# Start-up of a fused layernorm, scan and feed-forward kernel: other transposes in place of dummy matmuls, one copy on another engine, and a new order of the weight passes

## The chip, the cores and the metric

One core of one Trainium2 chip runs the whole program. The metric is the time of one execution on the device in microseconds (us), median of several runs. The profile belongs to one of the runs, and its clock starts with the span, which is some 1.3 us shorter than the time of the run.

## The reference, cut to what matters

```python
def reference(A_x, ..., B_w_gate, B_w_up, B_w_down):     # x: 1 x 2048 x 512, bf16
    def _A_ref(x, ...):            # diagonal complex state space model, P = 512
        Bu = einsum("bld,pd->blp", x + 0j, B_bar)
        h_t = Lam_bar * h_(t-1) + Bu_t                    # over 2048 steps
        return 2.0 * einsum("blp,dp->bld", hseq, Cmat).real + x * Dskip
    def _B_ref(x, w_gate, w_up, w_down):                  # F = 1376
        return (_gelu(x @ w_gate) * (x @ w_up)) @ w_down
    xn = _layernorm(A_x, axis=-1)
    return A_x + _A_ref(xn, ...) + _B_ref(xn, B_w_gate, B_w_up, B_w_down)
```

The 2048 rows go through in four blocks of four tiles (128 rows each). The change concerns only the first block, and of that only the first seven chunks of 128 columns of w_gate and w_up.

## The kernel before: the parts that the change touches

The program must start with TensorE while data is still coming in. Tile j of x is centred (the mean taken off, by VectorE), turned (four 128 x 128 transposes on TensorE into a PSUM bank), copied to SBUF, and then multiplied by the weights. The contraction over 512 is cut in four passes k = 0..3, because the weights arrive in four slices. `ks(k, j, w)` is pass k of tile j; `fill(n)` issues n small dummy matmuls, which stand in the queue so that TensorE stays active while it waits.

```python
        for k in range(KD):                       # loads, on the sync engine's queue
            if k in (1, 3):
                ld_x0((k + 3) // 2)               # x tiles 2 and 3
            ld_wk(WG, WGc, ins["B_w_gate"], k)    # slice k: 128 x 512, 128 KB
            ld_wk(WU, WUc, ins["B_w_up"], k)
# ... cut ...
        def cent_T(j, k0, k1, bank, eng="A", c0=0):          # turn, then copy
            ...
            PE(f, 56.0 * (k1 - k0), [XNp[j][k0 > 0] if j < 2 else XN[j], IDN], [BANK[bank]], "T0")
            ...
            if eng == "A":
                GATE["evTA"] = ACT(lambda e: e.activation(dst, src, ACTF.Copy, scale=sc), ...)
                return GATE["evTA"]
            return V(lambda e: e.tensor_scalar(dst, src, sc, None, ALU.mult), ...)
# ... cut ...
        ch(V(lambda e: e.tensor_reduce(SUM0.ap, X[0].ap, ...)))
        ch(cent(0, 0), cent(0, 1))
        fill(1)
        ch(cent_T(0, 0, 1, 7, "V"))
        ch(cent(1, 0), cent(1, 1))
        fill(4)
        # ks(k, j, w): pass k of tile j, for both column groups
        ks(0, 0, [0], True)
        cent_T(1, 0, 1, 6)
        ks(0, 0, [1])
        cent_T(0, 1, 4, 7)
        ks(0, 1, [0], True)
        cent_T(1, 1, 4, 5)
        ks(0, 1, [1])
        for j in range(2):
            ks(1, j, [0, 1])
        # ... statistics of tiles 0 to 3 on VectorE ...
        cent_T(2, 0, 4, 7)
        for j in range(2):
            ks(2, j, [0, 1])
        for k in range(3):
            ks(k, 2, [0, 1], k == 0)
        for j in range(3):
            ks(3, j, [0, 1])
            for u in range(2):
                GT_evac(j, u, acc(j, u))
            if j == 0:
                cent_T(3, 0, 4, 6)
        # then GT_mm: whole groups of four passes, later weights all there
```

After this block come, for every four tiles, the rest of the gate and up projection (GU), the state space input (BU), and the down projection (DN). GU and BU read x turned by DMA transposes (`TR`), not by TensorE.

## Time and profile before

| | before |
|---|---|
| time, median of 3 runs | 177.21 us (177.15 to 177.61) |
| span of the profiled run | 175.7 us |
| TensorE busy | 98% of the span, 98% of the chain that ended last |
| first real matmul | 4.57 us |
| start of pass k=1 / k=2 / first whole group | 6.06 / 7.42 / 11.10 us |

TensorE works almost without a hole. So the time can be read as three terms: the moment at which TensorE enters its unbroken stretch (the first whole group, line L711 before and L712 after), the work from there on, and whatever waits turn up in that stretch.

### The profile page before, as it was taken

What the parts mean: (1) busy time and instruction counts of PE and PEld (TensorE: products, weight loads), DVE (VectorE), ACT (ScalarE), POOL (GpSimd) and SP (SyncE); (2) the same over time, 40 slices, a digit from 0 to 9 for tenths busy, and PEclk for the clock granted to TensorE, in tenths of its full rate; (3) what the DMA queues carried; (4) which work ended last, traced back from release to release, by engine and by line L of the source; (5) the groups of instructions that cost most, each with busy time, mean ns of one, the idle gap of its engine ahead of it and who ended that gap; (6) DMA issues with size and microseconds to landing.
All of it is one profiled execution on the core that took longest, in us unless ns stands there. A gap on an engine that the chain in (4) does not pass through costs nothing.

```text
span 175.7 us, 2494 instructions
## 1 busy us (share of the span) xinstructions
PE 172.1 (98%) x868; PEld 84.0 (48%) x883; DVE 159.8 (91%) x279; ACT 95.5 (54%) x185; POOL 10.7 (6%) x24
## 2 busy tenths in 40 slices
PE   8999999999999999999999999999999999999995
PEld 3545564644544444444644444444464444444454
DVE  6987999996999989889899999989999899999941
ACT  5476677899876898383576792000667970000000
POOL 3122030201000000002100000000000000000000
DMA  5899999695998000002015000002001000000311
GB/s 155 241 320 174 215 178 222 126 132 113 191 298 225 0 4 2 0 30 85 8 39 111 1 0 0 4 0 90 30 0 30 4 0 0 0 0 0 120 64 60
DMA packets 32420, 14.36 MB, mean 82 GB/s; under 512 B 23736, under 2 KB 32408, under 8 KB 32408
## 3 DMA queue, kind: packets, MB, share of 16 engines
q1 hardware_dynamic: 32240, 14.07, 35.5%
q8 instruction: 7, 0.11, 0.3%
q10 hardware_dynamic: 168, 0.13, 0.2%
q14 instruction: 5, 0.04, 0.1%
HBM read 6.46 MB, written 2.10 MB: 49 GB/s over the span
## 4 chain that ended last, share of the span: by engine, by line
PE 98%; issue 1%; DVE 0%
PE PS L883 37%; PE PS L842 32%; PE PS L748 16%; PE PS L711 4%; PE PS L700 3%; PE PS L816 3%; PE PS L932 2%; PE PS L679 1%; PE PS L939 0%; DVE arena L901 0%
## 5 line engine op out<-in xcount | busy, mean ns | idle before, releaser
L883 PE MATMUL PS<-arena 128*128 128x512 bf16 (+3 forms) x317 | 65.9, 366 | 0.3
L842 PE MATMUL PS<-arena 128*128 128x512 bf16 x257 | 57.1, 379 | 0.4
L883 PEld LDWEIGHTS PS<-arena 128*128 128x128 bf16 (+1 forms) x323 | 30.8, 98 | 35.2
L842 PEld LDWEIGHTS PS<-arena 128*128 128x128 bf16 x264 | 25.8, 98 | 30.2
L786 DVE TENSOR_TENSOR_SCAN arena<-arena 128x512 bf16<-128x512 f32 x32 | 38.9, 1255 | 0.0
L857 ACT ACTIVATE arena<-PS 128x512 bf16<-128x512 f32 x33 | 19.8, 599 | 25.8 <-DVE arena L901 16.7
L748 PE MATMUL PS<-arena 128*128 128x512 bf16 (+1 forms) x134 | 28.0, 366 | 0.1
L861 ACT ACTIVATE arena<-PS 128x512 bf16<-128x512 f32 x33 | 19.8, 600 | 5.1 <-PE PS L842 5.1
L875 ACT ACTIVATE PS<-arena 128x512 f32<-128x512 bf16 (+2 forms) x17 | 9.6, 581 | 19.7 <-DVE arena L901 19.0
L748 PEld LDWEIGHTS PS<-arena 128*128 128x128 bf16 x136 | 13.3, 98 | 14.1
L757 ACT ACTIVATE arena<-PS 128x512 bf16<-128x512 f32 x32 | 17.7, 592 | 2.1 <-PE PS L748 2.1
L901 DVE TENSOR_TENSOR arena<-PS,arena 128x512 bf16<-128x512 f32 (+2 forms) x17 | 10.9, 653 | 6.4 <-PE PS L883 6.4
L863 DVE TENSOR_TENSOR arena<-arena 128x512 bf16<-128x512 bf16 x33 | 13.1, 416 | 1.7 <-ACT arena L861 1.6
L775 DVE TENSOR_TENSOR arena<-arena 128x4096 bf16<-128x4096 bf16 (+1 forms) x5 | 9.2, 1859 | 0.8 <-ACT arena L606 0.8
L773 DVE TENSOR_TENSOR arena<-arena 128x4096 bf16<-128x4096 bf16 (+1 forms) x5 | 9.2, 1859 | 0.1
L798 DVE TENSOR_TENSOR arena<-arena 128x4096 bf16<-128x4096 bf16 x4 | 9.2, 2288 | 0.1
L799 DVE TENSOR_TENSOR arena<-arena 128x4096 bf16<-128x4096 bf16 x4 | 9.1, 2284 | 0.0
L720 ACT ACTIVATE arena<-PS,arena 128x256 bf16<-128x256 f32 (+1 forms) x16 | 6.6, 448 | 3.9 <-PE PS L700 2.1
L610 DVE BATCH_NORM_STATS2 arena<-arena 128x6 f32<-128x512 bf16 x12 | 7.7, 679 | 0.1
L711 PE MATMUL PS<-arena 128*128 128x512 bf16 (+1 forms) x40 | 7.1, 336 | 0.0
L723 DVE SCALAR_TENSOR_TENSOR arena<-PS,arena 128x256 bf16<-128x256 f32 (+1 forms) x16 | 6.3, 445 | 0.5 <-PE PS L700 0.5
L700 PE MATMUL PS<-arena 128*128 128x512 bf16 (+1 forms) x28 | 6.2, 349 | 0.2
(96 smaller groups left out, 124.6 us busy)
## 6 DMA issues: line engine op xcount, KB each, us to landing
out_dram<-arena SPq DMA_DIRECT2D x15, 128.0 KB, 1.7
arena<-in_A_x_dram SPq DMA_DIRECT2D x3, 512.0 KB, 5.3
arena<-in_B_w_down_dram SPq DMA_DIRECT2D x1, 1280.0 KB, 7.2
arena<-in_B_w_gate_dram SPq DMA_DIRECT2D x4, 128.0 KB, 3.0
arena<-in_B_w_up_dram SPq DMA_DIRECT2D x4, 128.0 KB, 3.1
arena<-in_B_w_gate_dram SPq DMA_DIRECT2D x1, 480.0 KB, 6.5
arena<-in_B_w_up_dram SPq DMA_DIRECT2D x1, 480.0 KB, 7.4
arena<-arena SPq DMA_TRANSPOSE x25, 3.1
```

Of the source, the lines that this page charges most:

```text
L700: PE(lambda e: e.matmul(dst, XCd(j, k), WGU[:, ws[0]:ws[-1] + 1, k, f0:f1], start=first, stop=k == KD - 1, skip_group_check=True), d_pe([w ...
L711: ins_ = e.matmul(dst, XCd(j, k), WGU[:, :, k, f0:f1], start=(k == 0), stop=(k == KD - 1))
L748: ins_ = e.matmul(PS[bank][:, 128 * j0:128 * j1], BBT[c][dk].ap[:, 128 * s:128 * (s + 1)], XNT[b].ap[:, dk, 128 * j0:128 * j1], start=(dk ...
L757: GATE["evBu"] = ACT(lambda e, bank=bank, k3=k3, s=s, c=c: e.activation(SSc[k3][s][c].ap, PS[bank][:, :], ACTF.Copy), d_act(512), [BANK[ba ...
L786: V(lambda e, g=g, rb=rb, init=init: e.tensor_tensor_scan(g.ap, rb, g.ap, init, ALU.mult, ALU.add), d_dve_scan(512), [g, PA[RRr]] + ([CARc ...
L842: ins_ = e.matmul(PS[bank][0:m, c0:c1], W.ap[:, dk, 128 * ft:128 * ft + m], XNT[b].ap[:, dk, c0:c1], start=(dk == 0), stop=(dk == KD - 1))
L857: GATE["last_gelu"] = ACT(lambda e, bg=bg, kk=kk, m=m: e.activation(GG[kk].ap[0:m, :], PS[bg][0:m, :], ACTF.Gelu_apprx_tanh), d_act(512), ...
L861: ACT(lambda e, bu=bu, kk=kk, m=m: e.activation(UPB[kk].ap[0:m, :], PS[bu][0:m, :], ACTF.Copy), d_act(512), [BANK[bu]], [UPB[kk]], "evU")
L863: V(lambda e, kk=kk, m=m, ft=ft, k2=k2: e.tensor_tensor(HTt[k2][ft].ap[0:m, :], GG[kk].ap[0:m, :], UPB[kk].ap[0:m, :], ALU.mult), d_dve_tt ...
L875: ACT(lambda e: e.activation(PS[bank][:, c0:c1], X[tt].ap[:, c0:c1], ACTF.Copy), d_act(c1 - c0), [X[tt]], [BANK[bank]], "seed")
L883: ins_ = e.matmul(PS[bank][:, c0:c1], l_[:, 128 * j:128 * (j + 1)], r_[:, c0:c1], start=False, stop=last and n == len(ops) - 1, skip_group ...
L901: V(lambda e: e.tensor_tensor(OUTB[ko].ap[:, c0:c1], PS[bank][:, c0:c1], XD[tt].ap[:, c0:c1], ALU.add), d_dve_1x(c1 - c0), [BANK[bank], XD ...
```

## The change

Its intent is to keep TensorE on useful work while the first tiles and weights arrive: transposes that are needed anyway replace dummies, VectorE is relieved of a copy, and tile 2 is made ready early enough to fill the wait ahead of pass k=2.

```diff
+        fill(2)
+        cent_T(0, 0, 1, 7)                 # copy now by ScalarE
+        ch(cent(1, 0), cent(1, 1))
         fill(1)
-        ch(cent_T(0, 0, 1, 7, "V"))
-        ch(cent(1, 0), cent(1, 1))
-        fill(4)
+        ev0 = cent_T(0, 1, 4, 5, True)
+        ev1 = cent_T(1, 0, 1, 6)
+        S.order_behind(ev0(), ev1)
         ks(0, 0, [0], True)
-        cent_T(1, 0, 1, 6)
         ks(0, 0, [1])
-        cent_T(0, 1, 4, 7)
+        cent_T(1, 1, 4, 7)
         ks(0, 1, [0], True)
-        cent_T(1, 1, 4, 5)
         ks(0, 1, [1])
-        for j in range(2):
-            ks(1, j, [0, 1])
-        ch(*stats(0, 2)); ch(sub(2)); ch(*stats(0, 0)); ch(*stats(0, 1))
+        ch(*stats(0, 2)); ch(sub(2))
+        ks(1, 0, [0, 1])
+        cent_T(2, 0, 1, 6)
+        cent_T(2, 1, 4, 7)
+        ks(1, 1, [0, 1])
+        ks(0, 2, [0, 1], True)
+        ch(*stats(0, 0)); ch(*stats(0, 1))
 ... cut: statistics, norms ...
-        cent_T(2, 0, 4, 7)
-        for j in range(2):
+        ks(1, 2, [0, 1])
+        for j in range(3):
             ks(2, j, [0, 1])
-        for k in range(3):
-            ks(k, 2, [0, 1], k == 0)
         for j in range(3):
-            ks(3, j, [0, 1])
+            GT_k(3, j, 0, [0, 1])
+            if j == 0:
+                cent_T(3, 0, 4, 6)
+            GT_k(3, j, 1, [0, 1])
             for u in range(2):
                 GT_evac(j, u, acc(j, u))
-            if j == 0:
-                cent_T(3, 0, 4, 6)
 ... cut: banks of the first two groups of tile 3 swapped ...
```

More of the change, by code (lines that the diff above doesn't have):

```diff
@@ L671, in build, with cent_T @@
         XNp = [[Buf("XN%d_%d" % (j, n), "sb", XN[j].lo + 256 * n, XN[j].lo + (1024 if n else 256)) for n in range(2)] for j in range(2)]
-        def cent_T(j, k0, k1, bank, eng="A", c0=0):
-            pt = PS[bank].bitcast(BF16)[:, c0:c0 + 128 * (k1 - k0)]
+        def cent_T(j, k0, k1, bank, later=False):
+            pt = PS[bank].bitcast(BF16)[:, 0:128 * (k1 - k0)]
             def f(e):
@@ L684, in cent_T, with evac @@
             sc = 1.0 if j else 1.0 / D
-            if eng == "A":
+            def evac():
                 GATE["evTA"] = ACT(lambda e: e.activation(dst, src, ACTF.Copy, scale=sc), d_act(128 * (k1 - k0)), [BANK[bank]], w, "evT")
                 return GATE["evTA"]
-            return V(lambda e: e.tensor_scalar(dst, src, sc, None, ALU.mult), 110 + 0.6 * 128 * (k1 - k0), [BANK[bank]], w, "evT")
+            return evac if later else evac()
         FR = ((0, 256), (256, 512), (512, 768), (768, 896))
@@ L994, in build @@
         TR(0, [0, 1])
-        cent_T(2, 0, 4, 7)
-        for j in range(2):
+        ks(1, 2, [0, 1])
+        for j in range(3):
             ks(2, j, [0, 1])
-        for k in range(3):
-            ks(k, 2, [0, 1], k == 0)
         for j in range(3):
-            ks(3, j, [0, 1])
+            GT_k(3, j, 0, [0, 1])
+            if j == 0:
+                cent_T(3, 0, 4, 6)
+            GT_k(3, j, 1, [0, 1])
             for u in range(2):
                 GT_evac(j, u, acc(j, u))
-            if j == 0:
-                cent_T(3, 0, 4, 6)
         for (j, u), bank in zip([(3, 0), (3, 1), (0, 2), (0, 3), (1, 2), (1, 3), (2, 2), (2, 3), (3, 2), (3, 3)],
-                                (7, 6, 0, 1, 2, 3, 4, 5, 0, 7)):
+                                (6, 7, 0, 1, 2, 3, 4, 5, 0, 7)):
             GT_mm(j, u, bank)
```

## The prediction

> **What bounds the kernel now.** I read the page first, then the chain that ended last, then the timelines of matmuls (PE) and weight loads (PEld) in the first 12 us, which is all the change touches, and last the issue and landing of the weights' DMAs.
>
> ```profile
> PE 172.1 (98%) x868; PEld 84.0 (48%) x883; DVE 159.8 (91%) x279; ACT 95.5 (54%) x185; POOL 10.7 (6%) x24
> ...
> PE 98%; issue 1%; DVE 0%
> ```
>
> TensorE is busy for 98% of the span and carries 98% of the chain. So only three things shorten this kernel: less TensorE work, fewer TensorE stalls, a shorter tail. From 7.42 us on the chain is TensorE without a break; its pieces of 0.05 us "issue" are holes of one missing record (883 weight loads, 868 matmuls). What the change can win lies before that:
>
> ```profile
> 4.46 0.11 issue
> 4.57 0.38 PE PS L700 x2
> ...
> 7.34 0.08 issue
> 7.42 2.75 PE PS L700 x12
> ```
>
> The merged weight loads show where TensorE waits (bracket: idle before it, and what ended it):
>
> ```profile
> 4.54 0.13 PEld L700 LDWEIGHTS PS<-arena 128*128 128x128 bf16 x2 [0.26 <-issue]
> ...
> 5.37 0.11 PEld L700 LDWEIGHTS PS<-arena 128*128 128x128 bf16 x2 [0.15 <-ACT arena L686]
> ...
> 6.03 0.13 PEld L700 LDWEIGHTS PS<-arena 128*128 128x128 bf16 x2 [0.16 <-issue]
> ```
> ```profile
> 7.39 0.13 PEld L700 LDWEIGHTS PS<-arena 128*128 128x128 bf16 x2 [0.23 <-issue]
> ```
>
> "issue" hides two causes. At 6.03 it is the second ScalarE copy (5.42 to 5.91). At 7.39 it is a DMA: L700 accumulates over four passes (the code's steps k = 0..3), pass k needs slice k of both weights, and here pass k=2 begins. Issue and time to landing of the "up" slices k = 1, 2, 3:
>
> ```profile
> 3.07 0.43 SPq L484 DMA_DIRECT2D arena<-in_B_w_up_dram  x1
> ...
> 4.02 0.43 SPq L484 DMA_DIRECT2D arena<-in_B_w_up_dram  x1
> ...
> 5.45 0.43 SPq L484 DMA_DIRECT2D arena<-in_B_w_up_dram  x1
> ```
> ```profile
> arena<-in_B_w_up_dram SPq DMA_DIRECT2D x1, 128.0 KB, 2.8
> ```
> ```profile
> arena<-in_B_w_up_dram SPq DMA_DIRECT2D x1, 128.0 KB, 3.3
> ```
> ```profile
> arena<-in_B_w_up_dram SPq DMA_DIRECT2D x1, 128.0 KB, 3.8
> ```
>
> These landed at about 5.84, 7.29 and 9.25 us. Pass k=2 started at 7.42, that is 0.13 us after its slice. So **the start-up is paced by the weights' arrival**, and the next arrival is close too:
>
> ```profile
> 9.36 0.10 PEld L700 LDWEIGHTS PS<-arena 128*128 128x128 bf16 x1
> ```
>
> This is the first weight load of pass k=3. It ran 0.11 us after slice 3 landed; the loads that really stalled on a semaphore pair ran 0.10 us after it (7.39 after 7.29). Pass k=3 has almost no room.
>
> ```profile
> 7.42 2.75 PE L700 MATMUL PS<-arena 128*128 128x512 bf16 x12
> 10.01 0.39 PE L679 MATMUL PS<-arena 128*128 128x128 bf16 x4
> 10.23 1.03 PE L700 MATMUL PS<-arena 128*128 128x512 bf16 x4
> ```
>
> From these starts a 512-wide matmul takes (10.01-7.42)/12 = 0.216 us of TensorE, a turn (128x128 transpose) 0.22/4 = 0.056 us, a 256-wide one 0.109 us. Pass k=3 is the eleventh matmul after 7.42: 7.42 + 10 x 0.216 = 9.58 us.
>
> **What the Trainium skill says.** (1) "TensorE: Matmul & The Clock Gate", Part 1: the array starts at half clock and is released by some 3.4 us of sustained activity, on a free-running window. The trace agrees: the dummies of L932 are 0.427 us apart, twice 0.216, and the small dummies go from 0.107 to 0.074 us apart at 4.2 us, 3.4 us after the first. (2) The same page, Part 2, says LDWEIGHTS are pulled ahead of running matmuls. The trace agrees: the load at 9.36 starts with the matmul before its own. So a late semaphore costs only what exceeds one matmul. (3) The same page, Part 4: a transpose takes about 275 ns in a kernel and does not count as activity the same way. Here one lasts 218 to 286 ns from start to end; whether it counts no view shows. This speaks against swapping dummies for turns. (4) "ScalarE: Activation LUTs", What ACT_TABLE_LOAD costs: an activation with immediates takes 186 ns + 0.833 ns per element, 293 ns for 128. The trace has 277 for the copy, and 225 for VectorE's copy of the same shape.
>
> **The change, part by part.**
> - Dummies: five become three. Two go, each 0.107 us at the cold clock, but the three other turns of tile 0 and the first of tile 1 fill that time. The first real matmul waits for the copy of tile 0's first turn, not for dummies, so nothing is won directly.
> - That copy moves to ScalarE: +0.05 us (277-225), and about +0.05 us because a second dummy now stands ahead of the turn (it starts near 3.93, not 3.87). The first L700 matmul goes from 4.57 to about 4.67. Against that VectorE is free sooner, so tile 1 is centred by about 4.4 instead of 4.81.
> - Pass k=0 then runs without the wait of 0.15 us at 5.37: 4.67 + 8 x 0.109 + 3 turns 0.17 = 5.71 us. But slice 1 allows pass k=1 only at 5.84 + 0.13 = 5.98 (before: 6.06). Won: 0.08 us; 0.27 us are stall.
> - Tile 2's turns go ahead of k=2, with pass 0 and 1 of tile 2 (four 512-wide): 5.98 + 0.43 + 0.22 (turns) + 0.43 + 0.86 = 7.93 us. Pass k=2 starts there, after slice 2 (7.29), so **the 0.25 us wait at 7.42 goes**. Its six matmuls end at 7.93 + 1.29 = 9.22 us.
> - The work ahead of pass k=3 is the same as before (three passes for three tiles, 12 turns), only reordered. TensorE is ready at 9.22 instead of 9.58, 0.36 us sooner. But slice 3 landed at 9.25, and a stalled load plus its matmul follows 0.135 us after (7.29 to 7.42): 9.39 us. **Won: 9.58 - 9.39 = 0.19 us; the other 0.17 us become a new wait.**
> - Tile 3's turns one matmul sooner: before, their copy ended at 11.03 and the next group started at 11.10, with no stall but no room. If only pass k=3 came 0.19 sooner, this copy would be the limit. With the change the turns start at 9.60, the copy runs about 10.03 to 10.63, and the group starts at 9.39 + 1.29 + 0.22 = 10.90 without a wait. Cost: none; it protects the 0.19.
> - After that nothing is removed. In before, the L711 loads have at least 0.6 us of room to their weights (landed 11.94), the L842 loads after them 0.8 us, and the ones that wait for DMA transposes later 0.56 us. An advance of 0.19 us survives to the end, where TensorE drives the tail.
>
> Sum: 177.21 - 0.19 = 177.02 us, 0.1%.
>
> **Rivals.**
> 1. *All stalls go.* From 4.57 us on they sum to 0.15 + 0.07 + 0.03 + 0.25 = 0.50 us; this would give 176.7. Against it: the DMA queue issues without waits until 7.5 us, so no engine can make slices 1 and 3 come sooner. Room above my 0.19 exists only if slice 3 lands earlier in those runs; TensorE's own limit is 0.36 us (176.85).
> 2. *The wait only moves.* If slice 3 lands 0.1 to 0.2 us later than in this one profile, before barely pays (its slack is what I measured) or pays the same, and the gain falls to 0: 177.2. I hold a gain of 0 to 0.1 us for quite possible.
> 3. *The clock is released later*, since turns replace dummies around 4.2 us. Each 128-wide piece then costs 0.05 us more and each 256-wide one 0.107. For it: skill point 3. Against it: seven long dummies and two short ones still fill 0.77 to 3.93 us, and pass k=0 has 0.27 us to spare before slice 1. A delay of 0.3 us is absorbed; one of a whole window would cost over 1 us. I give that 4%.
> 4. *ScalarE becomes the bound*: it has all copies now, and tile 3's copy stands ahead of the first gelu, which moves from 10.06 to about 10.55. The first bank it frees is wanted only near 12.6 us, the product on VectorE being done by about 11.6. Hidden.
>
> **Range and chances.** The spread of before is 177.15 to 177.61, as large as any gain here. Centre 177.0; rivals 1 and 2 and the noise of a median give 176.75 to 177.3. A change of 2% is 3.5 us; the whole touched stretch has 0.5 us of stalls, so faster by over 2% is all but impossible, and slower needs a clock or a wait that I do not see.
>
> **What would show it.** In the profile after: pass k=0 starts near 4.67; a stall before pass k=1, then none before k=2; a weight load of pass k=3 held until about 0.1 us after slice 3 lands (idle of roughly 0.15 us there, ended by "issue" or a DMA); L711's first group near 10.90 and L842's first load near 17.7 instead of 17.91; span near 175.5. Wrong if the 128-wide pieces are still 0.107 us apart after 4.5 us, if a wait on ScalarE's copies appears ahead of tile 1's or tile 2's matmuls, or if pass k=3 starts without a stall (then the gain is larger).

## The result, and the profile after

| | before | changed |
|---|---|---|
| median of 6 runs | 177.19 us (177.06 to 177.61) | 177.68 us (177.35 to 178.32) |
| span of the profiled run | 175.7 us | 176.5 us |
| ratio | | 1.0031, 95% interval 1.0006 to 1.0055 |

A ratio is the mean time of one kernel's fast runs over that of the other's of the same rounds, so it is not quite the ratio of the medians. Within 2% the two are the same, as predicted, but 177.68 lies above the predicted range. The six runs of the changed kernel were 177.35, 177.36, 177.59, 177.77, 178.28 and 178.32 us; the profile is of the one at 177.77.

The page of the changed kernel gives busy time, share of the span and instructions of each engine, then the share of each in the chain that ended last:

```profile
PE 172.0 (97%) x866; PEld 83.9 (48%) x881; DVE 159.8 (91%) x278; ACT 95.0 (54%) x187; POOL 9.8 (6%) x24
...
PE 80%; DVE 6%; DMA 6%; SPq 4%; issue 2%; POOL 1%; DVEq 0%; POOLq 0%
```

TensorE's work is what it was (172.0 us against 172.1). But the chain has only 80% of TensorE, where it had 98%: something else ended a wait late in the program, and the chain runs back through it. That piece of the chain, in order of time (start, length, what):

```profile
26.72 2.46 DVE arena L599 x4
29.17 3.75 DMA arena<-arena
32.92 0.14 issue
33.06 3.62 PE PS L749 x20
```

At 29.17 us the fourth DMA transpose of x block 1 was issued; it landed at 32.92, and the BU matmuls of block 1 (L749) had to wait for it. In the kernel before, the chain has nothing but TensorE at this place:

```profile
26.90 9.03 PE PS L748 x49
```

The list of what the weight loads waited for, longest last column, shows that it was one wait:

```profile
PEld PS L749 <- DMA arena<-arena: 0.8, 1, 0.8
PEld PS L701 <- issue: 0.7, 1, 0.7
```

The idle time of the loads is not the loss itself: from the start of one matmul to the next, TensorE lost 0.72 us at L749, and 0.61 us at L701. The 0.72 us are nearly all of the 0.8 us by which this span is longer, and they lie some 20 us after the part that was changed. The transpose was late for two reasons. It was issued at 29.17 us, 0.5 to 1.0 us later than in seven of the nine other profiles below (the chain has its issue wait for VectorE, L599). And it took 3.75 us to land, against 2.46 to 3.43 us in those nine. The second line is the wait in the changed part, ahead of pass k=1. The timeline of weight loads there (start, length; in brackets the idle time before):

```profile
5.27 0.37 PEld L701 LDWEIGHTS PS<-arena 128*128 128x128 bf16 x4
6.34 0.13 PEld L701 LDWEIGHTS PS<-arena 128*128 128x128 bf16 x2 [0.70 <-issue]
...
7.77 1.73 PEld L701 LDWEIGHTS PS<-arena 128*128 128x128 bf16 x9 [0.21 <-ACT arena L687]
```

The change did what it was made for: pass k=0 runs on without the ScalarE wait, and nothing waits for slice 2 any more. From 7.77 us nine loads follow without a hole, across passes k=1 and k=2 of tile 2 and of the others; the 0.21 us of idle time ahead of them cost nothing between matmuls. But slice 1 of w_up landed at 6.28 us, not at the 5.84 of the profile before, and TensorE, ready at 5.76, stood for 0.61 us. Pass k=1 began at 6.38 against 6.06, and the first whole group at 11.14 against 11.10. So in this one pair of profiles the start-up won nothing, and the late transpose cost 0.72 us. The question was whether either is caused by the change.

### The profile page after: what moved, and what is told of

The parts are those of the page before. It is cut to its first block, busy times and chain, and to the rows that moved or that the text cites. A ratio compares the mean times of both kernels' runs of the same rounds, so it can differ in the third digit from the quotient of the medians.

```text
span 176.5 us, 2485 instructions
## 1 busy us (share of the span) xinstructions
PE 172.0 (97%) x866; PEld 83.9 (48%) x881; DVE 159.8 (91%) x278; ACT 95.0 (54%) x187; POOL 9.8 (6%) x24
## 3 DMA queue, kind: packets, MB, share of 16 engines
HBM read 6.46 MB, written 2.10 MB: 48 GB/s over the span
## 4 chain that ended last, share of the span: by engine, by line
PE 80%; DVE 6%; DMA 6%; SPq 4%; issue 2%; POOL 1%; DVEq 0%; POOLq 0%
PE PS L884 37%; PE PS L843 29%; PE PS L749 11%; DMA arena<-arena 6%; PE PS L817 2%; SPq L484 2%; DVE arena L599 1%; DVE arena L610 1%; SPq L489 1%; DVE arena L597 1%; DVE arena L629 1%; DVE arena L724 1%; SPq L493 1%; POOL arena L552 1%; DVE arena L864 0%
## 5 line engine op out<-in xcount | busy, mean ns | idle before, releaser
L749 PE MATMUL PS<-arena 128*128 128x512 bf16 (+1 forms) x134 | 28.2, 366 | 0.7 <-DMA arena<-arena 0.6
L749 PEld LDWEIGHTS PS<-arena 128*128 128x128 bf16 x136 | 13.2, 98 | 14.9 <-DMA arena<-arena 0.8
L721 ACT ACTIVATE arena<-PS,arena 128x256 bf16<-128x256 f32 (+1 forms) x16 | 6.1, 446 | 2.5 <-DVE arena L556 1.6
L712 PE MATMUL PS<-arena 128*128 128x512 bf16 (+1 forms) x40 | 7.1, 336 | 0.0
L701 PE MATMUL PS<-arena 128*128 128x512 bf16 (+1 forms) x28 | 6.0, 348 | 0.4 <-issue 0.4
```

The costliest lines, as they stand in the source:

```text
L749: ins_ = e.matmul(PS[bank][:, 128 * j0:128 * j1], BBT[c][dk].ap[:, 128 * s:128 * (s + 1)], XNT[b].ap[:, dk, 128 * j0:128 * j1], start=(dk ...
```

## The experiments

Sixteen kernels were run, in five timed rounds, which with the profiled run gives six times of each (five of one of them), with the kernel before beside them. Two theories stand against each other. *Chance of the transfers*: the landings of the same DMA differ from run to run, more than the change is worth; the changed kernel measured again comes out at or below the kernel before. *Cost of the change*: the earlier or different order delays the later transposes or the clock, so the changed kernel is slower by 0.3% again, and one of its halves shows it alone. The record names the chip for each of the four sets (6, 4, 0 and 11), but not for the first measurement, so that a difference between chips is not excluded.

### First set: both kernels again, and the halves

The first two have no edit but a comment line at the end.

> The changed kernel once more, unchanged. Theory 'late DMA' (in the profiled run of the changed kernel the input DMAs landed 0.3 to 0.6 us later than in the run before, from the first 128 KB on, and a matmul of the second BU waited 0.72 us for a DMA transpose of the next x block): if this is only that run's DMA, the ratio to before is 0.998 to 1.001 here, and the profile shows the third weight slice (k=2) near 7.3 us and no wait at 32 us. Theory 'the change costs': ratio 1.002 to 1.005 again, and again a wait in the second BU.

Measured: 177.17 us (176.99 to 177.33), ratio 0.9987 (0.9974 to 0.9999), with no wait at 32 us. (The expectation overstates the delay of the first profile: against the kernel before, the first loads landed within 0.1 us or so of each other; those from x tile 2 to slice 3 of w_gate landed 0.2 to 0.6 us later, and slice 3 of w_up 0.13 us earlier.)

> The kernel before against itself, for the noise and for a second profile of its DMAs. Both theories: ratio 1.000 within 0.1%. 'Late DMA': landings of the weight slices differ by 0.2 us or more from the first profile, in either direction. 'The change costs': they repeat within 0.1 us.

Measured: 177.73 us (177.09 to 177.91), ratio 1.0017 (1.0001 to 1.0034). The kernel before, against itself, came out slower, and the interval leaves 1 out. It follows that such an interval can leave out 1 even for two copies of one and the same program in the same rounds, and that the first measurement's 1.0031 has to be read with this.

The half that touches only the start:

```diff
 # start of the changed kernel (turns for dummies, copies by ScalarE),
-        ks(1, 0); cent_T(2, 0, 1, 6); cent_T(2, 1, 4, 7); ks(1, 1); ks(0, 2) ...
+        # but from pass 1 on the order of the kernel before
```

> Only the first half of the change: turns of tile 0 in place of two dummies, first turns copied by ScalarE; the order from step 1 on is that of before. 'The start costs' (the clock is released later without the dummies, or the DMAs are disturbed): 1.002 to 1.005. 'The order costs' or 'late DMA': 0.999 to 1.001.

Measured: 177.25 us (177.16 to 178.29), ratio 1.0001 (0.9981 to 1.0022). The group began at 11.15.

```diff
 # start of the kernel before (five dummies, copy by VectorE),
-        for j in range(2): ks(1, j, [0, 1]) ...
+        # but from pass 1 on the order of the changed kernel
```

> Only the second half: the start of before, tile 2 in two parts ahead of step 2, tile 3 turned a matmul sooner; VectorE's order of products and norms changes with it. 'The order costs' (products on VectorE later, so later norms of the second x block and later DMA transposes): 1.002 to 1.005. 'The start costs' or 'late DMA': 0.998 to 1.000, the 0.2 us of the prediction won or not.

Measured: 177.24 us (176.9 to 177.63), ratio 0.9991 (0.9976 to 1.0006). The group began at 11.27. Neither half costs 0.3%.

The second profile of the changed kernel shows the start as the prediction had it. Weight loads first, then matmuls, around pass k=3:

```profile
5.94 0.13 PEld L701 LDWEIGHTS PS<-arena 128*128 128x128 bf16 x2 [0.37 <-issue]
6.54 0.23 PEld L679 LDWEIGHTS PS<-arena 128*128 128x128 bf16 x4 [0.47 <-DVE arena L950]
...
9.52 0.10 PEld L701 LDWEIGHTS PS<-arena 128*128 128x128 bf16 x1 [0.49 <-issue]
```
```profile
9.15 0.78 PE L701 MATMUL PS<-arena 128*128 128x512 bf16 x2
9.77 0.38 PE L679 MATMUL PS<-arena 128*128 128x128 bf16 x4
9.99 1.24 PE L701 MATMUL PS<-arena 128*128 128x512 bf16 x5
11.07 0.59 PE L712 MATMUL PS<-arena 128*128 128x512 bf16 x2
```

Slice 1 came at 5.88 here, so pass k=1 began at 5.97. Nothing waits for slice 2. At 9.52 a weight load of pass k=3 was held, 0.10 us after slice 3 landed at 9.42. Two 512-wide matmuls that follow each other take 0.59 us (last row); the two at 9.15 took 0.78, so TensorE waited 0.19 us for slice 3. There is one wait more that the prediction had not priced: tile 2's turn at 6.54 waits for VectorE's centring (L950), which costs 0.14 us between matmuls.

In the kernel before, run again, slice 1 landed at 6.35:

```profile
6.41 0.56 PEld L700 LDWEIGHTS PS<-arena 128*128 128x128 bf16 x4 [0.48 <-issue]
7.08 0.42 PEld L679 LDWEIGHTS PS<-arena 128*128 128x128 bf16 x4
7.47 0.59 PEld L700 LDWEIGHTS PS<-arena 128*128 128x128 bf16 x4
```

Now pass k=2 (7.47) has no idle time before it at all: pass k=1 began late, and slice 2 was there when TensorE came to it. **The wait that the change removes is not in this run of the kernel before.**

### Second set: move a landing on purpose

If the landings of the slices set the start in both kernels, a load of 128 KB put ahead of slice 1 must cost both about the same.

```diff
             ld_wk(WU, WUc, ins["B_w_up"], k)
+            if k == 0:
+                S.dma(lambda e: e.dma_start(WD.ap[:, 0, :], ins["B_w_down"][0:128, :]), ...)
```

> The changed kernel with one more 128 KB load between weight slices 0 and 1, so that every later DMA is about 0.4 us later on purpose. Theory 'the start is paced by the weights and the second BU by a DMA transpose': slower by 0.3 to 0.8 us (1.002 to 1.0045 of before), stalls ahead of pass k=1 of 0.7 us or more and a wait in the second BU, as in the slow first profile of the changed kernel. Rival 'TensorE work paces it': within 0.1% of before.

Measured: 177.79 us (177.55 to 177.98), ratio 1.0024 (1.0011 to 1.0037).

> The kernel before with the same extra load. 'Late DMA makes both slow alike': 1.002 to 1.005 too, at most 0.3 us slower than the changed kernel with the load. Rival 'the changed order is what makes late DMAs costly': this one stays at 1.000 to 1.001 while the changed kernel with the load is slower by 0.3 us or more.

Measured: 177.68 us (177.49 to 178.12), ratio 1.0026 (1.0013 to 1.0038). Both kernels lost the same quarter of a per cent, 0.4 to 0.5 us by the ratios. The loads of the changed kernel with that delay, then those of the kernel before with it:

```profile
7.16 0.13 PEld L703 LDWEIGHTS PS<-arena 128*128 128x128 bf16 x2 [0.84 <-issue]
```
```profile
6.52 0.56 PEld L702 LDWEIGHTS PS<-arena 128*128 128x128 bf16 x4 [0.49 <-DMA arena<-in_B_w_gate_dram]
```

In both TensorE stands ahead of pass k=1. So the landings do set the start-up, and a start-up delay does come through to the end in both. (The two profiled runs are not alike in the landings: slice 1 of w_up came at 7.10 and 6.46 us, the second no later than in some runs without the load, and slice 2 at 7.75 and 7.74. The group began at 11.95 and 11.55. The timed runs decide.) The wait in the second BU that was expected for the changed kernel did not come.

Next, the block 1 transposes were issued ahead of a broadcast and a load of x, to test whether these two hold them up:

```diff
         def load_B():                                  # called ahead of TR(1)
             load_T(...)
+
+        def load_D():
             S.dma(... DSKB.ap, ins["A_Dskip"] ...)
             ld_x(2)
# ... cut ...
         TR(1)
+        load_D()
```

> The changed kernel with the four DMA transposes of the second x block ahead of the loads of the skip vector and of x block 2. 'The runs of 178.3 come from the second BU waiting for these transposes': no run above 177.7, transposes landed by 29 us, no wait in the second BU, median 177.0 to 177.2. Rival 'the slow runs come from the start alone': the spread of the changed kernel (177.0 to 178.3) stays.

Measured: 177.72 us (176.98 to 178.14), ratio 1.002 (1.0 to 1.0041). This failed its purpose: the profiled run, at 178.14, was slow by another transpose, the fourth of x block 0, which landed at 18.93, 4.1 us after issue. Three of six runs lay above 177.7 us, where none was expected, so slow runs have at least one cause besides block 1. For block 1 the one profile does show an effect: its four transposes took 2.42 to 2.48 us each from issue to landing, against 2.46 to 5.97 us in the ten profiles of the two kernels. But the fourth was issued at 28.80 us and landed at 31.28, no sooner than elsewhere, so nothing was won.

Last of the set, slice 1 of w_up was issued from ScalarE's queue, early:

```diff
-            ld_wk(WU, WUc, ins["B_w_up"], k)
+            if k == 1:
+                GATE["par"] = S.order_behind(ld_wk(WU, WUc, ins["B_w_up"], k, "scalar"), GATE["par"])
+            else:
+                ld_wk(WU, WUc, ins["B_w_up"], k)
```

> The changed kernel with the up slice k=1 issued from ScalarE's queue about 1.6 us earlier, so that the later slices are issued 0.47 us earlier too. 'Issue of the weights paces the start': slice 1 lands near 5.4 us, slice 3 near 8.9 us, the stalls ahead of pass k=1 and k=3 (0.28 and 0.19 us in the second profile of the changed kernel) shrink below 0.1 us in sum, median 0.2 to 0.4 us below the changed kernel (ratio to before 0.996 to 0.998). Rival 'the DMA engines' bandwidth paces it': the slices land as before and nothing is won.

Measured: 177.35 us (176.73 to 177.99), ratio 1.0003 (0.9984 to 1.0022). Slice 1 of w_up came at 4.93 us, and slices 2 and 3 came sooner too (6.82 and 8.58 us, against 7.10 to 7.57 and 8.92 to 9.59 in the ten profiles). But slice 0 came later (5.14 us, against 3.90 to 4.79), and so did the gate's slice 1 (6.17, against 5.29 to 5.50):

```profile
5.18 0.11 PEld L704 LDWEIGHTS PS<-arena 128*128 128x128 bf16 x2 [0.39 <-DMA arena<-in_B_w_up_dram]
...
6.22 0.11 PEld L704 LDWEIGHTS PS<-arena 128*128 128x128 bf16 x2 [0.32 <-DMA arena<-in_B_w_gate_dram]
...
6.86 0.23 PEld L682 LDWEIGHTS PS<-arena 128*128 128x128 bf16 x4 [0.53 <-DVE arena L953]
```

The wait moved to these two slices and to VectorE's centring of tile 2 (last line), and the group began at 11.21. Neither theory had it: the slices did not land as before, and nothing was won.

### Third set: no later slices to wait for

With a wrong result, every pass reads slice 0, so passes k = 1 to 3 never wait for weights.

```diff
# cut at the dots
-            PE(lambda e: e.matmul(dst, XCd(j, k), WGU[:, ws[0]:ws[-1] + 1, k, f0:f1], ...),
-               ..., [(WGc, WUc)[w_][k] for w_ in ws] + ...)
+            PE(lambda e: e.matmul(dst, XCd(j, k), WGU[:, ws[0]:ws[-1] + 1, 0, f0:f1], ...),
+               ..., [(WGc, WUc)[w_][0] for w_ in ws] + ...)
```

> Wrong result on purpose: the changed kernel with passes k=1..3 multiplying slice 0 of the weights again, so that they wait for no later slice. 'The slices' arrival takes the gain': without it the changed order starts pass k=3 0 to 0.3 us before the other kernel's without it (next run), no stall ahead of k=1 or k=3; ahead of tile 2's turn a wait for VectorE's centring, which follows the landing of x tile 2, of up to 0.5 us. Rival 'the change costs engine time of its own': it starts pass k=3 later than the next run.

Measured: 177.11 us (176.76 to 177.97), ratio 0.9993 (0.9969 to 1.0017); the group began at 10.89. With no slice to wait for, the wait for VectorE's centring of tile 2 is the next limit:

```profile
6.54 0.23 PEld L679 LDWEIGHTS PS<-arena 128*128 128x128 bf16 x4 [0.68 <-DVE arena L950]
```

> Wrong result on purpose: the same in the kernel before. Both theories: the stall ahead of k=2 is gone, pass k=3 starts near 9.3 to 9.4 us instead of 9.6, median 0 to 0.3 us below before; later waits (weights of columns 512 on, landing near 12 us; transposes of x block 1) may take some of it.

Measured: 176.99 us (176.78 to 177.75), ratio 0.9987 (0.9963 to 1.0011). In its profiled run the clock was released only near 5.8 us and the group began at 11.45, so the profiles of the two don't compare, and the times don't tell them apart. This pair is inconclusive about the difference of the two orders. It does suggest how little any order can win here: with all slices there at once the ratios are still within about 0.1% of 1, and both intervals include 1.

> The changed kernel a third time. 'No effect beyond the DMAs' run-to-run difference' (first measurement 1.0031, second 0.9987): 0.998 to 1.002; over the three measurements the mean ratio is within 0.1% of 1. 'The change costs': 1.002 or more.

Measured: 177.11 us (176.96 to 177.47), ratio 0.9991 (0.9971 to 1.001).

> The kernel before against itself a second time, for the noise (first such ratio: 1.0017, interval 1.0001 to 1.0034, although nothing differs): 0.998 to 1.002.

Measured: 177.30 us (177.12 to 177.93), ratio 1.0002 (0.9981 to 1.0023). Its profile shows a late release of the clock in the kernel before, with all five dummies. The first pair of 256-wide matmuls there, and below it the same pair in the first profile of that kernel:

```profile
4.54 0.58 PE L700 MATMUL PS<-arena 128*128 128x256 bf16 x2
```
```profile
4.57 0.38 PE L700 MATMUL PS<-arena 128*128 128x256 bf16 x2
```

A late release is thus no effect of the missing dummies. It was seen in both kernels.

### Fourth set: more looks at both

What was still open: how often slow runs come with each kernel, and whether the wait for slice 2 is a rule or an exception in the kernel before. No edits but a comment line.

> The changed kernel a fourth time. 'Slow runs are DMA differences that any of the kernels meets': ratio 0.998 to 1.002, at most one run of six above 178.1. 'The changed order makes slow runs more frequent': about two of six above 178.1, as in its first measurement.

Measured: 177.09 us (176.87 to 177.36), ratio 0.9981 (0.9957 to 1.0006).

> The changed kernel a fifth time; the same two theories and numbers as for the fourth. Over the three of this call: at most one run of 18 above 178.1, or about six.

Measured: 177.14 us (176.91 to 177.33), ratio 0.9984 (0.9962 to 1.0007).

> The kernel before against itself a third time: 0.998 to 1.002; with its rounds, 17 more runs of the kernel before, of which by 'DMA differences that any kernel meets' about one lies above 178.0 (so far 1 of 51), and by 'the changed order makes them' none above 178.1.

Measured: 177.24 us (177.1 to 177.77), ratio 0.9996 (0.9972 to 1.002). Here the wait ahead of pass k=2 is back:

```profile
7.53 2.29 PEld L700 LDWEIGHTS PS<-arena 128*128 128x128 bf16 x12 [0.20 <-issue]
```

> The changed kernel a sixth time; the same two theories and numbers as for the fourth. In its profile pass k=3 starts 0.135 us after slice 3 lands, and the first group of tile 3 starts 1.52 us after that, in 11.0 to 11.15 us.

Measured: 177.16 us (176.94 to 177.81), ratio 0.9989 (0.9964 to 1.0013). The profile fell on the slowest run, 177.81, and its chain shows why:

```profile
14.54 4.12 DMA arena<-arena
18.65 0.14 issue
18.79 5.34 PE PS L843 x24
```

This time it is the fourth transpose of x block 0, issued at 14.54 and landed at 18.65; in the first profile of the kernel before the same transpose was issued at 14.48 and landed at 16.99. TensorE lost 0.79 us to it, at GU. The start was not as expected: slice 3 came early (8.92 us), pass k=3 waited for nothing, and it was the late slice 1 that set the group's start, 11.08.

Of the 18 runs of the changed kernel in this set none lay above 178.1 us, where "the changed order makes slow runs more frequent" expected about six; of the 17 of the kernel before one did, 178.47.

### What the ten profiles of the two kernels say together

Times in us from the span's start. "Start of the group" is the first matmul of L711 (before) or L712 (changed). The waits, and what a late transpose cost, are taken from one matmul's start to the next.

| kernel, run | slices 1, 2, 3 of w_up landed | pass k=1 | start of the group | waits ahead of k=1, k=2, k=3 | late transpose | time |
|---|---|---|---|---|---|---|
| before, first | 5.84, 7.29, 9.25 | 6.06 | 11.10 | 0.07, 0.25, 0 | none | 176.98 |
| before, second | 6.35, 7.24, 9.36 | 6.44 | 11.20 | 0.39, 0, 0 | none | 177.09 |
| before, third | 5.73, 7.37, 9.39 | 6.47 | 11.23 | 0.23, 0, 0 | none | 177.12 |
| before, fourth | 6.17, 7.42, 9.34 | 6.26 | 11.23 | 0.29, 0.21, 0 | none | 177.11 |
| changed, first | 6.28, 7.57, 9.12 | 6.38 | 11.14 | 0.61, 0, 0 | 0.72 | 177.77 |
| changed, second | 5.88, 7.25, 9.42 | 5.97 | 11.07 | 0.28, 0, 0.19 | none | 176.99 |
| changed, third | 5.74, 7.17, 9.36 | 5.83 | 11.01 | 0.26, 0, 0.27 | none | 176.99 |
| changed, fourth | 6.56, 7.26, 9.25 | 6.65 | 11.41 | 0.63, 0, 0 | none | 177.36 |
| changed, fifth | 6.40, 7.10, 9.59 | 6.49 | 11.25 | 0.76, 0, 0 | none | 177.16 |
| changed, sixth | 6.22, 7.30, 8.92 | 6.32 | 11.08 | 0.69, 0, 0 | 0.79 | 177.81 |

Two rules fit all of them to a few hundredths. Let P be the start of pass k=1. The kernel before starts the group at the later of P + 4.76 and (slice 2) + 3.81; the changed kernel at the later of P + 4.76 and (slice 3) + 1.65. The constants are the work that is left: 20, 16 and 6 matmuls of 0.216 us, with eight, four and four turns of 0.056 us, and for the last two the 0.13 us by which a stalled matmul follows its slice. The rules hold as well for the profiles of e3 to e7, from which they were not made: they give 11.15, 11.27, 11.95, 11.55 and 11.26, and so it was measured. When pass k=1 begins late, both kernels have the same term, P + 4.76, and the change wins nothing. It wins where slice 2 lands more than 4.76 - 3.81 = 0.95 us after P. Putting each profile's own landings and P into both rules gives a gain of 0.20, 0, 0 and 0.21 us for the four of the kernel before, and of 0.24, -0.01, -0.03, 0, 0 and 0.03 us for the six of the changed kernel: 0.06 us in the mean, an estimate. (It takes P as the same in both kernels, which leaves out the ScalarE wait in pass k=0.) The measured mean starts of the group, 11.19 for four profiles and 11.16 for six, agree with so small a gain. All four profiles of the kernel before are of runs below its median of 177.30, so they may show it in its better half.

From the last matmul of L711 or L712 to the last matmul of the program it is 155.69 us in all eight profiles without a late transpose, in both kernels; in the two others it is 156.41 and 156.47.

Over all runs the changed kernel has 36, with a mean of 177.26 us and a median of 177.17; the kernel before has 68, with 177.37 and 177.30. Runs above 177.7 us: 4 of 36 with the change, 9 of 68 without, up to 178.32 and 178.47; above 178.1 us, 2 of 36 and 1 of 68. None of the slow runs of the kernel before was profiled, so that a late transpose made them slow too is argued, not shown. Nor is the issue of block 1's transposes later with the change: the first was issued at 24.34 to 24.80 us before, and at 24.43 to 24.89 with it. Five of the six measurements of the changed kernel have medians of 177.09 to 177.17, inside the predicted range; the first has 177.68.

## Why the prediction was right or wrong

Two steps of the prediction failed. "Won: 9.58 - 9.39 = 0.19 us" took the landings of one profile as fixed; in the profiled run slice 1 came at 6.28 us, not 5.84, TensorE waited 0.61 us for it, and the group began 0.04 us later than before, not 0.19 sooner. And "an advance of 0.19 us survives to the end" trusted in the 0.56 us of room that one DMA transpose had in one profile; in that run the transpose used it up and cost 0.72 us more. Point by point:

- **The class was right**: within 2%, by TensorE being busy for 98% of the span.
- **"So the 0.25 us wait at 7.42 goes"**: right. None of the six profiles of the changed kernel has a wait ahead of pass k=2.
- **"The other 0.17 us become a new wait"** ahead of pass k=3: right in mechanism and size where slice 1 is as early as it was taken (0.19 and 0.27 us with slice 1 at 5.88 and 5.74). A stalled matmul followed 0.135 us after its slice, as used: 9.42 to 9.55. In the other four the wait sits ahead of pass k=1 instead, and pass k=3 waits for nothing; the prediction had taken that as a sign of a larger gain, but it came with none. Its sum was right for its own landings: with slice 3 at 9.25 the rule gives the predicted 10.90.
- **"Won: 9.58 - 9.39 = 0.19 us"**: this term was mis-sized. It took the landings of one profile as fixed. Slice 1 landed anywhere from 5.73 to 6.56 us, and the wait of 0.25 us exists only where pass k=1 begins early beside slice 2: in two of four profiles of the kernel before. With the rules above the mean is 0.06 us. Rival 2 ("the wait only moves", a gain of 0 to 0.1 us) had the right reason in part: the landings vary. It looked for the variation in slice 3; slice 1 had more of it.
- **"An advance of 0.19 us survives to the end"**, with 0.56 us of room to the DMA transposes: this step failed in the profiled run. The fourth transpose of x block 1 landed at 32.92 us, against 31.1 to 31.9 in the nine other profiles, so the room was used up and 0.72 us more lost. In the sixth profile another transpose did the same, at GU (0.79 us). The room had been read from one landing, like the slices.
- **The range** had no place for this: "Centre 177.0; rivals 1 and 2 and the noise of a median give 176.75 to 177.3". The noise was taken from three runs. One late transpose adds 0.7 to 0.8 us to a run, which is four times the gain, and nothing in the range stood for it. The kernel before, unchanged, had medians from 177.19 to 177.73 in its eight groups of runs.
- **Rival 3** (clock released later because turns replace dummies): no case for it. The release came between 3.7 and 5.3 us in the six profiles with the change and between 3.6 and 5.5 in the four without. What a late one costs depends on the landings. In the changed kernel's fourth profile (5.3 us) all of it was spent waiting for slice 1. In the third of the kernel before (5.5 us) pass k=1 began 0.74 us after slice 1, 0.14 us after ScalarE's copy for it, but only 0.05 us of this came through, as slice 2 allowed the group no sooner than 11.18. With no slice to wait for (e10, 5.8 us), the group began 0.56 us later than in e9, though these two differ in the order as well.
- **Rival 4** (ScalarE becomes the bound): not seen. Tile 3's turn a pass sooner left no wait on its copy; in all four profiles of the kernel before, the loads of L711 come with some 0.3 us of such idle time, without cost between matmuls. Rival 1 (all stalls go) was not seen either: 0.26 to 0.76 us ahead of pass k=1 stay in all six profiles.
- **Left out of the prediction**: tile 2's turn waits for VectorE's centring, 0.14 us in the two profiles with an early slice 1 and up to 0.36 us with all slices there. With slice 1 as late as in the other four it is hidden.

What stays open: why the first measurement lay half a microsecond above the five later ones, with two runs at 178.28 and 178.32. Its one profile, at 177.77, has a late transpose that accounts for 0.72 us of that run; the other five runs, the two slowest among them, were not profiled. Slow runs are not more frequent with the change over all runs, so no cost of the change is shown. Nor is it settled what the change is worth: 0.06 us as the landings say, 0.11 us as the means over all runs say, or 0.16 to 0.34 us as the ratios of the five repeats say, each of which lies below 1 (0.9981 to 0.9991). The kernel before came out 0.3 us from itself, so none of these is clear of the noise. And why a transpose lands late in some runs was not found; the one experiment made for it shortened the flights of block 1's transposes in its one profile and met another late one.

## What to carry to other kernels

When start-up is paced by transfers, a wait that one profile shows is a sample: look at the landings in several profiles before pricing its removal, and write the start as the later of several landings plus the work behind each, which tells at once when a reorder pays. Reordering moved a wait from one pass to another here, as predicted where the landings were as taken, but the gain was smaller than what one late DMA transpose costs a run (0.7 to 0.8 us), and to see it needs many runs of both kernels. For a change of 0.1%, widen the range by what a repeat of the unchanged kernel shows.

## What the Trainium skill lacked or had wrong

- "TensorE: Matmul & The Clock Gate", Part 1, puts the release of the clock around 4 us of sustained activity, give or take 500 ns from run to run. Here activity began at 0.77 to 0.78 us in the same way in all 18 profiles. Read from the distances between matmuls, the release came between about 3.6 us (second profile of the kernel before: a dummy begun at 3.29 took 0.386 us, not 0.427) and 6.1 us (e5: 256-wide pieces still 0.213 us apart until 6.08), 2.9 to 5.4 us later: a wider spread than that sentence gives, in both kernels.
- "DMA: Bandwidth & Descriptors", Latency and other measured facts, gives figures for latency and none for how far a landing moves between executions of one program. Here slice 1 of w_up (128 KB) landed at 5.73 to 6.56 us, and one DMA transpose between SBUF tiles took 2.5 us in one run and 4.1 us in another. For a kernel with TensorE at 98% these decided more than the change.
